# Explicit per-engine instruction lists for a fused attention and MLP kernel

## The chip, the cores and the metric

The kernel runs on one core of a Trainium2 chip. The metric is the device time of one execution in microseconds, as a median of several runs. The core has five engines that take their instructions from queues of their own, each strictly in order: TensorE (PE, matrix products), ScalarE (ACT, functions such as exp), VectorE (DVE, elementwise work), GpSimd (POOL) and SyncE (SP), which here only issues transfers. An instruction at the head of a queue that waits for another engine holds everything behind it in that queue. So the order within each queue, which is fixed when the program is built, decides how well the engines overlap.

## What is computed

Eight batches, eight heads, 576 tokens, head size 64. A small packed set of 32 queries `p` attends to the keys and values, its result serves as keys and values for the queries `q`, and the result of that goes through an MLP with a swish whose slope is a vector.

```python
def sm_attn(qq, kk, vv):
    s = scale * np.matmul(qq, kk.transpose(0, 1, 3, 2))
    s = s - np.max(s, axis=-1, keepdims=True)
    a = np.exp(s)
    a = a / (np.sum(a, axis=-1, keepdims=True) + 1e-09)
    return np.matmul(a, vv)
p_packed = sm_attn(p, k, v)              # p: 8 x 8 x 32 x 64
out = sm_attn(q, p_packed, p_packed)     # q: 8 x 8 x 576 x 64
# x = out as (8*576) x 512
h = x @ w_in                             # 4608 x 2048
g = h * (1.0 / (1.0 + np.exp(-beta * h)))
y = g @ w_out                            # 4608 x 512
```

All inputs and the output are float32.

## The kernel before

The kernel multiplies `p_packed` into `w_in` first (tile `w_ps`, scaled by beta into `W_bf`), so that per batch `h_ps` is a product of `W_bf` and the attention weights `A2T`. It does 512 of a batch's 576 tokens as a main part and joins the remaining 64 of two batches (`hr_ps`, `g_rem`). For batches 2 to 7 the output product is one level of a seven-product scheme with sums of quarters of `w_out` (`w_sum`) and of `g` (`g_sum`); batches 0 and 1 use plain products, batch 0 in two halves of `w_out`.

Every piece of work is a task with a key, such as `("A2", 1, 0)`, an engine or several to choose from, an estimated duration, and the tasks that it depends on. The names that matter here:

- `ld`, `ld_in`, `ld_out`: loads of q, k, v and the two weights; `cast`: float32 to bf16 of q, k, v; `w_in`, `w_out`: casts of the weights; `tr`: transposes of k and q (by DMA from batch 2 on)
- `s1`, `e1`, `z1`, `pun`, `pp`: scores, exp, sums, product and normalisation of the first attention; `s2`, `e2`, `z2`, `l2`, `n2`, `A2`: the same of the second
- `w`, `W`: product of `pp` with `w_in`, and its scaling; `h`, `g`: first MLP product and its silu; `hr`, `gr`: the same for the remaining tokens
- `o`: plain output products; `p`, `P`: the seven products; `S`, `T4`: sums of `g` and of `w_out`; `take`, `add`, `R..`: reading the output out of PSUM

A planner turns the tasks into the five queues. It plays the program through in a time model, and each time an engine is free it takes the ready task with the lowest rank:

```python
while todo:
    moved = False
    for e in ready:
        if free[e] > now + 1e-9:
            continue
        can = [t for t in ready[e] if t.ready <= now + 1e-9 and room(t.takes, t.count) and best(t, e)]
        # ... (ScalarE: function tables are switched here)
        if not can:
            if e == "PE" and warm - 1e-9 <= now < WARM_UNTIL and room("o", 1):
                self.filler()                  # a small matmul on no data of the problem
                free[e], warm = now + 0.06, now + WARM_US
                moved = True
            continue
        start(min(can, key=lambda t: t.rank), e)
        moved = True
    # ... (nothing moved: step to the next time)
```

The ranks are a formula by batch and kind plus a table of numbers, one for each task, that an earlier search left; a second table holds back some tasks, a third ties some to one engine:

```python
ORDER = { ('A2', 0, 0): 89.4, ('A2', 0, 1): -16.1, ('A2', 0, 2): -98.7, ... }   # some 900 numbers
AFTER = { ('A2', 6, 1): 184.56, ('P', 2, 2): 109, ... }
PIN = { ('R11', 5): 'DVE', ('cast', 1, 'k', 2): 'ACT', ... }

def task(self, key, engine, us, fn, deps=(), rank=0, **kw):
    deps = [self.tk.get(d) if isinstance(d, tuple) else d for d in deps]
    t = self.plan.add(engine, us, fn, deps, rank + ORDER.get(key, 0), **kw)
    t.key, t.ready = key, AFTER.get(key, 0.0)
    if key in PIN:
        t.any = {PIN[key]: t.any[PIN[key]]}
```

The casts of q, k and v for batches 2 to 7 are GpSimd's, one instruction for all eight heads and one for the remaining tokens:

```python
c0 = self.task(("cast", b, x, 0), "POOL", 1.95, lambda f=piece: f("POOL", 0, 8), [m0] + old, rank + 3)
self.tk["cast", b, x, 1] = c0
self.task(("cast", b, x, 2), "POOL", 0.4, lambda f=tail: f("POOL"), [mr, c0], rank + 3)
```

The four sums of `w_out` (`w_sum`) need all of `w_out` cast, and are read first by the products of batch 2. `A2` multiplies two tiles in SBUF; `W` reads one operand from PSUM:

```python
a, b = {1: (w(0, 1), w(0, 0)), 2: (w(1, 1), self.sum_w(1)), 3: (w(1, 1), w(0, 1)), 4: (w(1, 0), self.sum_w(2))}[i]
nc.vector.tensor_tensor(self.sum_w(i), a, b, ALU.subtract)                    # T4
nc.vector.tensor_tensor(part(st[b, "A2"], i), part(st[b, "E2"], i), ..rz2.., ALU.mult)   # A2
nc.vector.tensor_tensor(st[b, "W"][:, r, cols], st[b, "w", m][:], self.beta_bc[:, cols], ALU.mult)   # W
# h of batch b needs A2 (b, 0), A2 (b, 1), two of the eight W of batch b, and the bank ring "h" of two
```

PSUM is dealt out in rings: two banks for `h`, two for `o`, four for the attention (`att`). A task that opens a bank waits until the one that had it has been read out.

Of the kernel before, what the change touches and what calls it, by code (L numbers as in the profile page):

```python
# [8 lines left out]
B, H, S, D = 8, 8, 576, 64  # L9
# [6 lines left out]
bf16 = mybir.dt.bfloat16  # L16
# [27 lines left out]
HALVED = (0,)  # L44
PLAIN = (0, 1)
# [3 lines left out]
ORDER = {  # L49
    ('A2', 0, 0): 89.4, ('A2', 0, 1): -16.1, ('A2', 0, 2): -98.7, ('A2', 1, 0): 0.2, ('A2', 1, 1): -1,  # L50
    ('A2', 2, 0): 100, ('A2', 2, 1): 70, ('A2', 2, 2): 70, ('A2', 3, 0): -22, ('A2', 3, 1): -23.7, ('A2', 3, 2): -19,
    ('A2', 4, 0): -16.6, ('A2', 4, 1): -3, ('A2', 4, 2): 72, ('A2', 5, 0): 7.7, ('A2', 5, 1): 5.4, ('A2', 5, 2): 3.7,
    ('A2', 6, 0): -36.4, ('A2', 6, 1): -66.7, ('A2', 6, 2): -10.7, ('A2', 7, 0): 185.4, ('A2', 7, 1): -153.6,
    ('A2', 7, 2): -86.6, ('P', 2, 1): -5.7, ('P', 2, 2): -0.9, ('P', 2, 4): -7, ('P', 2, 5): -474.2,
    ('P', 2, 6): -1.8, ('P', 2, 7): -462.9, ('P', 3, 2): 6.4, ('P', 3, 3): -14.7, ('P', 3, 4): -32.4,
    ('P', 3, 5): -33, ('P', 3, 6): -455.7, ('P', 3, 7): -464.5, ('P', 4, 1): 0.6, ('P', 4, 2): -464.5,
    ('P', 4, 3): -110.3, ('P', 4, 5): 5.1, ('P', 4, 6): -457, ('P', 4, 7): -439.9, ('P', 5, 1): -75,
    ('P', 5, 4): -433.3, ('P', 5, 5): 0.6, ('P', 5, 6): -461.4, ('P', 5, 7): -400.6, ('P', 6, 1): 7,
    ('P', 6, 2): -582.1, ('P', 6, 3): 25.1, ('P', 6, 5): -573.1, ('P', 6, 6): -514.9, ('P', 6, 7): -65.7,
    ('P', 7, 1): -67.6, ('P', 7, 2): 6.1, ('P', 7, 3): 0.6, ('P', 7, 4): -18, ('P', 7, 5): -0.9, ('P', 7, 6): 3.7,  # L60
    ('R11', 2): 78, ('R11', 3): -87, ('R11', 4): 97.2, ('R11', 5): 30.3, ('R11', 6): -6.4, ('R11', 7): 30.6,
    ('R11+', 2): -30.6, ('R11+', 3): 54.4, ('R11+', 4): 135.6, ('R11+', 5): 18.8, ('R11+', 6): 123, ('R11+', 7): 18.3,
    ('R12', 2): -42.6, ('R12', 3): -15, ('R12', 4): 0.7, ('R12', 5): -31.9, ('R12', 6): -1.3, ('R12', 7): -8.6,
    ('R12+', 2): 37, ('R12+', 3): -80.4, ('R12+', 4): 45, ('R12+', 5): 30, ('R12+', 6): 95, ('R12+', 7): -123.6,
    ('R21', 2): -121, ('R21', 3): 14, ('R21', 4): 30, ('R21', 5): -9.3, ('R21', 6): -53, ('R21', 7): 60,
    ('R22', 2): 0.3, ('R22', 3): 62.3, ('R22', 4): -1.7, ('R22', 5): -16.7, ('R22', 6): 9.4, ('R22', 7): -28.2,
    ('R22+', 2): -9.4, ('R22+', 3): 15.6, ('R22+', 4): -16, ('R22+', 5): 13.8, ('R22+', 6): 0.6, ('R22+', 7): 3,
    ('S', 2, 1): -12, ('S', 2, 2): -10.7, ('S', 2, 3): -5, ('S', 2, 4): -12, ('S', 3, 1): -4.3, ('S', 3, 2): -34.3,
    ('S', 3, 3): 2.7, ('S', 3, 4): -64.3, ('S', 4, 1): -61.3, ('S', 4, 2): -99.3, ('S', 4, 3): -106.3,
    ('S', 4, 4): -109.3, ('S', 5, 1): -235.9, ('S', 5, 2): 60, ('S', 5, 3): 83, ('S', 5, 4): 57, ('S', 6, 2): 60,  # L70
    ('S', 6, 3): 60.3, ('S', 6, 4): 57, ('S', 7, 1): 68.6, ('S', 7, 2): 71.6, ('S', 7, 3): 71.6, ('S', 7, 4): -3.4,
    ('T', 0, 'k', 0): 75, ('T', 0, 'k', 1): 75, ('T', 0, 'q', 0): 76.3, ('T', 0, 'q', 1): 75, ('T', 1, 'k', 0): 60.6,
    ('T', 1, 'k', 1): 90.6, ('T', 1, 'q', 0): 60.6, ('T', 1, 'q', 1): 60.6, ('T4', 1): -210.4, ('T4', 2): -73.5,
    ('T4', 3): -72.8, ('T4', 4): 15, ('W', 0, 0): -31.7, ('W', 0, 1): -30, ('W', 0, 2): -30, ('W', 0, 3): -30,
    ('W', 0, 4): -23, ('W', 0, 5): -30, ('W', 0, 6): 75.6, ('W', 0, 7): -11, ('W', 1, 0): -2.4, ('W', 1, 1): -35.1,
    ('W', 1, 2): 25, ('W', 1, 3): -90, ('W', 1, 4): -60, ('W', 1, 5): -53, ('W', 1, 6): -60.6, ('W', 1, 7): -60,
    ('W', 2, 0): -118.7, ('W', 2, 1): 57, ('W', 2, 2): 1.3, ('W', 2, 3): -30, ('W', 2, 4): 3, ('W', 2, 5): -60,
    ('W', 2, 6): -1.9, ('W', 2, 7): 13.7, ('W', 3, 0): -61.7, ('W', 3, 1): -61.7, ('W', 3, 2): -61.7,
    ('W', 3, 3): -30.4, ('W', 3, 4): -68.7, ('W', 3, 5): -91.7, ('W', 3, 6): -58.7, ('W', 3, 7): -60.4,
    ('W', 4, 0): 13, ('W', 4, 1): 73, ('W', 4, 2): -2, ('W', 4, 3): 12.4, ('W', 4, 4): 13.6, ('W', 4, 5): 13,  # L80
    ('W', 4, 6): -161.4, ('W', 4, 7): 28, ('W', 5, 0): 30, ('W', 5, 1): 26, ('W', 5, 2): 40.6, ('W', 5, 3): 30,
    ('W', 5, 4): 37, ('W', 5, 5): 30, ('W', 5, 6): 37, ('W', 5, 7): 31.3, ('W', 6, 0): 46, ('W', 6, 1): 84.3,
    ('W', 6, 2): 24.3, ('W', 6, 3): 54.3, ('W', 6, 4): -65.7, ('W', 6, 5): -49.3, ('W', 6, 6): 54, ('W', 6, 7): 51.7,
    ('W', 7, 0): 63, ('W', 7, 1): -57, ('W', 7, 2): 3, ('W', 7, 3): 3, ('W', 7, 4): 3, ('W', 7, 5): 3, ('W', 7, 6): 3,
    ('W', 7, 7): 3, ('add', 0, 0): 36.6, ('add', 0, 1): 70.8, ('add', 0, 2): 52, ('add', 0, 3): 37, ('b_safe',): 11,
    ('bcol',): -7, ('beta', 0): 67, ('beta', 1): 50, ('beta', 3): 36.4, ('brow', 0): 16.6, ('brow', 1): 14,
    ('brow', 2): -38.6, ('brow', 3): 180, ('cast', 0, 'k', 0): -80.9, ('cast', 0, 'k', 1): -49.2,
    ('cast', 0, 'k', 2): -73.9, ('cast', 0, 'q', 0): -13.9, ('cast', 0, 'q', 1): -80.3, ('cast', 0, 'q', 2): -80.9,
    ('cast', 0, 'v', 0): -78.3, ('cast', 0, 'v', 1): -20.9, ('cast', 0, 'v', 2): -83.9, ('cast', 1, 'k', 0): -76.7,
    ('cast', 1, 'k', 1): -76.7, ('cast', 1, 'k', 2): -76.7, ('cast', 1, 'q', 0): -76.7, ('cast', 1, 'q', 1): -83.7,  # L90
    ('cast', 1, 'q', 2): -147.4, ('cast', 1, 'v', 0): -23.9, ('cast', 1, 'v', 1): -76.7, ('cast', 1, 'v', 2): -76.7,
    ('cast', 2, 'k', 0): 88.7, ('cast', 2, 'k', 2): 28.7, ('cast', 2, 'q', 0): -1.3, ('cast', 2, 'q', 2): 29.3,
    ('cast', 2, 'v', 0): 58.7, ('cast', 2, 'v', 2): 31.7, ('cast', 3, 'k', 0): -0.7, ('cast', 3, 'k', 2): 1.2,
    ('cast', 3, 'q', 0): 0.6, ('cast', 3, 'q', 2): 37.6, ('cast', 3, 'v', 0): 7.9, ('cast', 3, 'v', 2): 60.6,
    ('cast', 4, 'k', 0): -53.6, ('cast', 4, 'k', 2): 3.4, ('cast', 4, 'q', 0): 6.4, ('cast', 4, 'q', 2): 8.3,
    ('cast', 4, 'v', 0): 21.4, ('cast', 4, 'v', 2): -38.6, ('cast', 5, 'k', 0): -5.3, ('cast', 5, 'k', 2): 60.4,
    ('cast', 5, 'q', 0): -25.9, ('cast', 5, 'q', 2): 31.7, ('cast', 5, 'v', 0): -43.3, ('cast', 5, 'v', 2): -1.9,
    ('cast', 6, 'k', 0): -16.3, ('cast', 6, 'k', 2): -0.7, ('cast', 6, 'q', 0): -1.3, ('cast', 6, 'q', 2): -1.3,
    ('cast', 6, 'v', 0): -1.3, ('cast', 6, 'v', 2): -15.7, ('cast', 7, 'k', 0): 7.6, ('cast', 7, 'k', 2): 0.6,
    ('cast', 7, 'q', 0): 0.6, ('cast', 7, 'q', 2): -14.4, ('cast', 7, 'v', 0): 0.6, ('cast', 7, 'v', 2): 0.6,  # L100
    ('e1', 0, 0): -61.9, ('e1', 0, 1): -1.9, ('e1', 1, 0): -326, ('e1', 1, 1): -326.3, ('e1', 2, 0): 26.1,
    ('e1', 2, 1): -391, ('e1', 3, 0): -59, ('e1', 3, 1): -44, ('e1', 4, 0): 98, ('e1', 4, 1): -4, ('e1', 5, 1): 13.7,
    ('e1', 6, 0): -30.7, ('e1', 6, 1): -31.3, ('e1', 7, 0): 60.6, ('e1', 7, 1): 60, ('e1r', 0): 68, ('e1r', 1): -29.4,
    ('e1r', 2): -388, ('e1r', 3): -11.4, ('e1r', 4): -60.6, ('e1r', 5): 5.3, ('e1r', 6): -38.9, ('e1r', 7): -32,
    ('e2', 0, 0): 7, ('e2', 0, 1): 69.8, ('e2', 1, 0): -68.3, ('e2', 1, 1): -7.3, ('e2', 2, 0): 41.1,
    ('e2', 2, 1): 48.7, ('e2', 3, 0): -6.4, ('e2', 3, 1): -375.3, ('e2', 4, 0): -80.9, ('e2', 4, 1): -80.3,
    ('e2', 5, 0): 67, ('e2', 5, 1): 7, ('e2', 6, 0): -46.2, ('e2', 6, 1): -46.5, ('e2', 7, 0): 52.4,
    ('e2', 7, 1): -14.6, ('e2r', 0, 0): -7.7, ('e2r', 0, 1): -8.3, ('e2r', 1, 0): 53.3, ('e2r', 1, 1): -3.7,
    ('e2r', 2, 0): -47.4, ('e2r', 2, 1): -47.4, ('e2r', 3, 0): -58.7, ('e2r', 3, 1): -58.1, ('e2r', 4, 0): 5.1,
# [177 lines left out]
    ('w', 3, 2): 99.46, ('w', 6, 1): 175.13, ('w', 6, 2): 183.08, ('w', 7, 1): 203.14,  # L287
}
PIN = {
    ('R11', 5): 'DVE', ('cast', 1, 'k', 2): 'ACT', ('w_in', 0, 1): 'POOL', ('w_out', 4): 'DVE',  # L290
}


# [17 lines left out]
class Planner:  # L311
# [14 lines left out]
    def run(self):  # L326
# [4 lines left out]
        for t in self.tasks:  # L331
            t.left = len(t.deps)
            for d in t.deps:
                d.users.append(t)
# [1068 lines left out]
```

## Time and profile before

| what | value |
|---|---|
| time, median of 3 runs | 260.38 us (260.34 to 261.25) |
| span of the profiled execution | 259.6 us |
| TensorE matmul busy | 235.8 us, 91% |
| ScalarE busy | 173.5 us, 67%, of which 26 table loads 33.4 us |
| VectorE busy | 162.0 us, 62% |
| GpSimd busy | 53.0 us, 20% |
| moved by DMA | 54.11 MB, mean 208 GB/s |

A profile's page cuts the span into 40 slices of 6.5 us and gives for each engine a digit, its busy share in tenths; a second row gives the clock that TensorE was granted. Other views answer for one stretch of time: busy time by stage, a timeline of the instructions of an engine (start, length, what it is, and in brackets how long the engine had been idle before it and what ended that), the waits summed by who waited for whom, and the chain of waits that ended last. Matmuls overlap one another, so a busy TensorE isn't one at its peak; idle time of an engine that isn't the bound costs nothing.

### The profile page before, as it was taken

What the parts mean: (1) busy time and instruction counts of PE and PEld (TensorE: products, weight loads), DVE (VectorE), ACT (ScalarE), POOL (GpSimd) and SP (SyncE); (2) the same over time, 40 slices, a digit from 0 to 9 for tenths busy, and PEclk for the clock granted to TensorE, in tenths of its full rate; (3) what the DMA queues carried; (4) which work ended last, traced back from release to release, by engine and by line L of the source; (5) the groups of instructions that cost most, each with busy time, mean ns of one, the idle gap of its engine ahead of it and who ended that gap; (6) DMA issues with size and microseconds to landing.
All of it is one profiled execution on the core that took longest, in us unless ns stands there. A gap on an engine that the chain in (4) does not pass through costs nothing.

```text
span 259.6 us, 5648 instructions
## 1 busy us (share of the span) xinstructions
PE 235.8 (91%) x2338; PEld 149.1 (57%) x2367; DVE 162.0 (62%) x245; ACT 173.5 (67%) x311; POOL 53.0 (20%) x51
## 2 busy tenths in 40 slices
PE   3995897785999999999999999999999999999993
PEld 2972344541344454478468646677567845767971
DVE  5768587999826546467637783664577488522621
ACT  3266749975286686688778878877786768656210
POOL 4022200038233006303510550054400000000000
PEclk9999999998699999999999999999999999999998
DMA  6999999999949599979969993998994021103122
GB/s 204 322 362 378 376 286 285 328 286 232 280 146 213 134 293 310 211 200 305 229 169 297 296 168 112 308 278 206 277 176 89 3 83 81 42 3 141 63 78 83
DMA packets 74825, 54.11 MB, mean 208 GB/s; under 512 B 42688, under 2 KB 68304, under 8 KB 74800
## 3 DMA queue, kind: packets, MB, share of 16 engines
q1 hardware_dynamic: 74496, 53.68, 78.0%
q8 instruction: 18, 0.29, 0.5%
q10 hardware_dynamic: 304, 0.07, 0.1%
q14 instruction: 7, 0.06, 0.1%
HBM read 37.23 MB, written 9.44 MB: 180 GB/s over the span
## 4 chain that ended last, share of the span: by engine, by line
PE 71%; DMA 14%; DVE 5%; ACT 5%; SPq 2%; POOL 1%; issue 1%
PE o_ps L448 40%; PE h_ps L448 19%; DMA w_in<-in_moe_w_in_dram 8%; DMA w_out<-in_moe_w_out_dram 5%; PE w_ps L448 3%; PE hr_ps L448 2%; DVE w_sum L1046 2%; DMA k<-in_k_dram 2%; PE s_ps L448 2%; PE z_ps L448 2%; ACT L463 1%; PE pp_ps L448 1%; ACT g_main L894 1%; POOL w_in_bf L1310 1%; DVE W_bf L862 1%
## 5 line engine op out<-in xcount | busy, mean ns | idle before, releaser
L894 ACT ACTIVATE g_main<-h_ps 128x512 bf16<-128x512 f32 x128 | 72.8, 596 | 40.1 <-PE h_ps L448 35.0
L448 PEld LDWEIGHTS <-g_main 128*128 128x128 bf16 x608 | 56.6, 98 | 31.5 <-issue 9.0
L448 PE MATMUL o_ps<-w_out_bf,g_main 128*128 128x256 bf16 (+1 forms) x409 | 72.5, 309 | 2.2 <-DVE w_out_bf L1321 1.6
L448 PE MATMUL h_ps<-A2T,W_bf 128*128 128x512 bf16 x238 | 70.4, 386 | 3.3 <-ACT g_main L894 1.5
L862 DVE TENSOR_TENSOR W_bf<-w_ps,beta_bc 128x512 bf16<-128x512 f32 x64 | 41.6, 684 | 15.5 <-PE w_ps L448 15.0
L448 PEld LDWEIGHTS <-W_bf 128*128 128x128 bf16 x512 | 32.4, 98 | 24.1 <-issue 10.5
L463 ACT ACT_TABLE_LOAD x26 | 33.4, 1283 | 1.1 <-PEq L1387 0.7
L448 PE MATMUL o_ps<-w_sum,g_main 128*128 128x256 bf16 x192 | 26.5, 273 | 0.2
L1102 DVE TENSOR_TENSOR o_sb<-o_ps,o_sb 128x512 f32<-128x512 f32 x18 | 12.4, 689 | 22.3 <-PE o_ps L448 17.3
L448 PE MATMUL o_ps<-w_sum,g_sum 128*128 128x256 bf16 x192 | 25.1, 273 | 0.1
L531 POOL CAST q_bf<-q 128x2048 bf16<-128x2048 f32 x6 | 11.9, 1988 | 46.4 <-DMA q<-in_q_dram 26.2
L448 PEld LDWEIGHTS <-g_sum 128*128 128x128 bf16 x192 | 18.4, 98 | 4.3 <-issue 0.2
L1104 DVE COPY o_sb<-o_ps 128x512 f32<-128x512 f32 x13 | 9.0, 690 | 17.1 <-PE o_ps L448 17.1
L448 PE MATMUL w_ps<-w_in_bf,pp 64*32 64x512 bf16 x256 | 13.7, 386 | 4.9 <-DVE W_bf L862 2.0
L448 PEld LDWEIGHTS <-pp 64*32 64x32 bf16 x384 | 5.6, 89 | 20.2 <-issue 16.8
L803 DVE TENSOR_TENSOR A2T<-E2T,rz 128x512 bf16<-128x512 bf16 x16 | 12.2, 770 | 6.6 <-ACT rz L798 6.6
L448 PE MATMUL o_ps<-w_out_bf,g_rem 128*128 128x512 bf16 x61 | 15.5, 380 | 0.4 <-ACT o_sb L1104 0.2
L531 POOL CAST v_bf<-v 128x2048 bf16<-128x2048 f32 x6 | 11.6, 1931 | 14.2 <-PE pp_ps L448 5.5
L531 POOL CAST k_bf<-k 128x2048 bf16<-128x2048 f32 x6 | 11.6, 1934 | 11.7 <-DMA k<-in_k_dram 10.0
L914 ACT ACTIVATE g_rem<-hr_ps 128x512 bf16<-128x512 f32 x16 | 9.5, 598 | 5.3 <-PE hr_ps L448 5.2
L1104 ACT COPY o_sb<-o_ps 128x512 f32<-128x512 f32 x11 | 6.4, 585 | 8.6 <-PE o_ps L448 8.5
L1072 DVE TENSOR_TENSOR g_sum<-g_main 128x2048 bf16<-128x2048 bf16 x6 | 7.3, 1220 | 7.6 <-ACT g_main L894 7.6
(96 smaller groups left out, 267.2 us busy)
## 6 DMA issues: line engine op xcount, KB each, us to landing
out_dram<-o_sb SPq DMA_DIRECT2D x14, 512.0 KB, 3.0
k<-in_k_dram SPq DMA_DIRECT2D x6, 1024.0 KB, 8.8
v<-in_v_dram SPq DMA_DIRECT2D x6, 1024.0 KB, 7.7
q<-in_q_dram SPq DMA_DIRECT2D x6, 1024.0 KB, 7.8
w_in<-in_moe_w_in_dram SPq DMA_DIRECT2D x4, 1024.0 KB, 8.4
w_out<-in_moe_w_out_dram SPq DMA_DIRECT2D x4, 1024.0 KB, 10.6
k<-in_k_dram SPq DMA_DIRECT2D x4, 512.0 KB, 7.3
q<-in_q_dram SPq DMA_DIRECT2D x4, 512.0 KB, 6.9
```

Source lines behind the costliest of these rows:

```text
L448: return self.nc.tensor.matmul(out, lhsT, rhs, start=start, stop=stop, tile_position=pos, skip_group_check=True)
L463: self.nc.scalar.preload_act_table_set(SETS[mode])
L531: self.copy[engine](o[:, 0:2048].rearrange("p (t h d) -> p h t d", t=4, h=8)[:, h], t[:, 0:2048].rearrange("p (h t d) -> p h t d", h=8, t= ...
L803: nc.vector.tensor_tensor(part(st[b, "A2"], i), part(st[b, "E2"], i), st[b, "rz2"][:, i] if i < 2 else st[b, "rz2r"][:], ALU.mult)
L862: nc.vector.tensor_tensor(st[b, "W"][:, r, cols], st[b, "w", m][:], self.beta_bc[:, cols], ALU.mult)
L894: nc.scalar.activation(st[b, "g"][:, ft, :], st[b, "h", ft][:], AF.Silu)
L914: nc.scalar.activation(st[b // 2, "gr"][:, 8 * half : 8 * half + 8, o : o + 64], st[b, "hr", half][:].rearrange("p (f n) -> p f n", f=8), ...
L1046: nc.vector.tensor_tensor(self.sum_w(i), a, b, ALU.subtract)
L1072: nc.vector.tensor_tensor(o, x, y, op)
L1102: nc.vector.tensor_tensor(o, x, o, ALU.add)
L1104: self.copy[engine](o, x)
L1310: self.copy[engine](self.w_in_bf[:, c, 512 * n : 512 * n + 512], self.t["w_in", n][:, c])
```

## The change

The tables of ranks, delays and ties go. In their place stands one list of task keys for each engine, found by a search over sequences. The planner takes each engine's tasks in the order of its list, and keeps a time model only to interleave the five lists when it writes the program and to place fillers in TensorE's gaps. The model, which the search used too, now knows that VectorE's work within SBUF (the kinds in `PORT`) and GpSimd's work exclude each other. The GpSimd casts of batches 2 to 7 are cut in two halves of four heads. Some dependencies that the old planner got from its order by rank are now stated.

```diff
+PORT = ("S", "T4", "A2", "cast", "w_in", "w_out", "p_dup", "p0_bf")
-ORDER = { ... }
-AFTER = { ... }
-PIN = { ... }
+SEQUENCE = {
+    "PE": [ ("brow", 0), ("tr", 0, "k", 0), ("p0_tr", 0), ("brow", 1), ... ],
+    ...
+    "DVE": [ ...
+        ("take", 0, 3), ("W", 1, 0), ("w_out", 12), ("w_out", 15), ("w_out", 14), ("W", 1, 1), ("rq", 1),
+        ("add", 0, 1), ("A2", 1, 0), ("A2", 0, 2), ("add", 0, 0), ("A2", 1, 1), ("W", 1, 2), ("W", 1, 3), ("T4", 1),
+        ("W", 1, 4), ("W", 1, 5), ("add", 0, 2), ("add", 0, 3), ("T4", 2), ("pT1", 0), ("W", 1, 6), ("pT1", 0, 1),
+        ("A2", 1, 2), ("pT1", 1, 1), ("T4", 3), ("W", 1, 7), ... ],
+    "POOL": [ ... ],
+    "SP": [ ... ("ld_out", 1), ("ld_in", 3), ("ld", 1, "q", 0), ("ld", 1, "v", 0), ("ld", 1, "v", 1), ("ld", 1, "v", 2),
+        ("ld", 1, "q", 1), ("ld_out", 2), ("ld_out", 3), ("ld", 1, "q", 2), ("ld", 2, "k", 0), ("ld", "p"),
+        ("ld", 2, "v", 0), ("ld", 2, "k", 2), ("ld", 2, "q", 0), ("ld", 2, "q", 2), ("ld", 2, "v", 2),
+        ("tr", 2, "k", 0), ... ],
+}
     # Planner.run
+        named = {t.key: t for t in self.tasks}
+        todo = {e: [named.pop(k) for k in keys] for e, keys in SEQUENCE.items()}
+            if e == "POOL":
+                at = max(at, held["DVE"] - 0.12)
+            elif e == "DVE" and t.port:
+                at = max(at, held["POOL"] - 0.12)
+            for _ in range(int((min(at, WARM_UNTIL) - free["PE"]) / WARM_US)):
+                self.filler()
     # casts of batches 2 to 7
-                c0 = self.task(("cast", b, x, 0), "POOL", 1.95, lambda f=piece: f("POOL", 0, 8), [m0] + old, rank + 3)
-                self.tk["cast", b, x, 1] = c0
+                c0 = self.task(("cast", b, x, 0), "POOL", 0.97, lambda f=piece: f("POOL", 0, 4), [m0] + old, rank + 3)
+                self.task(("cast", b, x, 1), "POOL", 0.97, lambda f=piece: f("POOL", 1, 4), [m0, c0], rank + 3)
     # dependencies now stated, for example
-                [h, ("g", b, 0) if ft else None], rank, ends=[h], table="silu",
+                [h], rank, ends=[h], table="silu",
```

Compared as instruction orders, the two programs have the same matmuls except for the fillers (70 before, 38 after), 26 and 24 table loads on ScalarE, 183 and 174 rows on VectorE, 56 and 68 on GpSimd. In the old order of VectorE three of the four `w_sum` come before the first `A2` of batch 1; in the new one both `A2` and four of the eight `W` of batch 1 come before the first `w_sum`. On the load queue the tensor p of the later batches moves from before the last two quarters of `w_out` to behind them.

## The prediction

> **What bounds the kernel now.** I read the page's slices first, then busy time by stage, then the timeline of VectorE and GpSimd in the one stage that stood out, then the chain of waits. The slices (6.5 us each):
>
> ```profile
> PE   3995897785999999999999999999999999999993
> ...
> PEclk9999999998699999999999999999999999999998
> DMA  6999999999949599979969993998994021103122
> ```
>
> TensorE is full from about 66 us to the end; before that it has holes in nearly every slice, and the clock row dips once, in slices 10 and 11 (58 to 71 us). The weights and the first two batches come in over the first 52 us, with the DMA row at 9. Busy time by stage (columns: length, then busy us and count of PE, PEld, DVE, ACT, POOL, then clock, DMA share, GB/s):
>
> ```profile
> 40.00:54.00 14.00, 10.14 (x130) 6.54 (x130) 11.78 (x23) 12.20 (x19) 1.05 (x2) 1.00 1.09 305
> 54.00:65.00 11.00, 7.83 (x92) 3.16 (x91) 10.97 (x13) 7.70 (x17) 7.08 (x6) 0.90 1.19 250
> ...
> 100.00:150.00 50.00, 49.59 (x540) 32.65 (x530) 32.45 (x47) 38.98 (x73) 15.77 (x15) 1.00 1.02 249
> ```
>
> From 54 to 65 us VectorE is busy 10.97 of 11 us: it, and no longer the loads, is the bound there. The same view in steps of 2 us shows what follows:
>
> ```profile
> 60.00:62.00 2.00, 0.40 (x8) 0.12 (x7) 1.98 (x4) 1.29 (x3) 1.31 (x2) 1.00 1.07 311
> 62.00:64.00 2.00, 1.04 (x9) 0.30 (x9) 2.00 (x2) 0.00 (x0) 1.87 (x2) 0.68 1.48 114
> 64.00:66.00 2.00, 1.98 (x6) 0.62 (x5) 2.00 (x3) 0.60 (x1) 1.66 (x1) 0.50 1.18 281
> 66.00:68.00 2.00, 2.00 (x6) 0.66 (x5) 2.00 (x3) 0.73 (x2) 0.23 (x1) 0.50 0.81 257
> 68.00:70.00 2.00, 2.00 (x7) 0.78 (x6) 1.13 (x3) 0.47 (x1) 0.40 (x1) 0.61 0.85 228
> ```
>
> TensorE stands still (0.40 of 2 us), and then runs at half clock until about 69 us. Lost to the clock: 0.32 x 2 + 0.5 x 4 + 0.39 x 2 = 3.4 us. The timelines of VectorE and GpSimd say why VectorE is late:
>
> ```profile
> 55.95 1.21 DVE L1046 TENSOR_TENSOR w_sum<-w_out_bf,w_sum 128x2048 bf16<-128x2048 bf16 x1
> 57.09 2.90 DVE L1046 TENSOR_TENSOR w_sum<-w_out_bf 128x2048 bf16<-128x2048 bf16 x1
> ...
> 60.63 0.68 DVE L803 TENSOR_TENSOR A2T<-E2T,rz 128x512 bf16<-128x512 bf16 x1
> ...
> 61.83 1.78 DVE L803 TENSOR_TENSOR A2T<-E2T,rz 128x512 bf16<-128x512 bf16 x1
> ```
> ```profile
> 56.78 2.14 POOL L531 CAST k_bf<-k 128x2048 bf16<-128x2048 f32 x1 [2.76 <-DMA k<-in_k_dram]
> 58.87 1.39 POOL L541 CAST k_bf<-kr 128x256 bf16<-128x256 f32 x1
> 60.95 2.12 POOL L531 CAST v_bf<-v 128x2048 bf16<-128x2048 f32 x1 [0.69 <-DMA v<-in_v_dram]
> ```
>
> The same operation takes 1.21 us alone and 2.90 us beside a GpSimd cast, 0.68 and 1.78 us for the other. In the chain of waits these pieces follow one another, w_sum for 3.96 us, W_bf, A2T for 1.70 us, and only at 63.66 us the h_ps that starts the dense part.
>
> **What the Trainium skill says.** "SBUF — State Buffer", section "SBUF: two separate sides", says that VectorE and GpSimd share a port pair as an exclusive lock, taken by a VectorE operation with two SBUF inputs or in a two-port mode; the loser waits for the other's whole instruction. The trace agrees (the pairs above; W_bf, which reads PSUM, stays at 0.69 us beside a cast). "TensorE: Matmul & The Clock Gate", Part 1, says the clock falls to half after idleness and comes back after a busy window of some 3.4 us; here it is 0.50 after the 2 us hole and back after some 6. "ScalarE: Activation LUTs", section "What ACT_TABLE_LOAD costs", gives 1283 ns; the trace has 1283.
>
> **The change, part by part.**
>
> *Same work.* By the two instruction orders, TensorE does the same matmuls but for fillers, 38 against 70. ScalarE has 24 table loads for 26 (2 x 1.28 = 2.6 us less), VectorE 174 rows for 183: three more w_out casts go to ScalarE, the small bias arithmetic and one cast of p to GpSimd. None of this is the bound after 66 us.
>
> *Casts in halves.* 18 GpSimd casts of 1.9 us become 36 of 128x1024, which the trace has once undisturbed at 1.04 us: +0.2 us each pair, 3.4 us in all on an engine at 20%, so free. A VectorE operation then waits at most about 1 us, not 1.9.
>
> *VectorE's order between 50 and 66 us.* Now all of w_out is cast, three w_sum are made (5.3 us), and then come W_bf and A2T of batch 1, on which h of batch 1 waits. The list puts both A2T and four of the eight W_bf of batch 1 ahead of the first w_sum; the four w_sum are spread over batch 1, since batch 2 reads them first.
>
> *When h of batch 1 can start.* In the loads' order p (384 KB) moves behind w_out, 1.3 us at 300 GB/s; VectorE first waited for the last w_out until 52.49 us, so estimate 51.2. Behind it the list has on VectorE three w_out at 0.44, W_bf 0.6, a small copy 0.25, two adds and two A2T at 0.6, a small A2T 0.2: 1.3 + 0.6 + 0.25 + 2.4 + 0.2 = 4.8 us, so 56.0. The list alternates with TensorE and ScalarE here (an add waits for its product, the product two tiles on waits for the bank the add frees, A2T for the logarithm and exponential of about 0.6 us each), some six hand-overs of 0.2 to 0.3 us: estimate **57 to 59, I take 58**. TensorE has products of batch 0 to do meanwhile, so it should not cool.
>
> *What remains then.* Before, the last matmul ends at 255.2 us. From 66 us on that is 189.2 us, of which 1.0 + 0.8 us were lost to the clock: 187.4 at full clock. By counts, what the old order had done at 66 and the new order has not when h of batch 1 starts: two or three h matmuls (0.5), 32 hr (0.94), 16 transposes of p (0.9); the other way, some eight output matmuls (1.7). Net +0.6: 188.0 us. 58 + 188.0 = 246.0, plus the tail after the last matmul as now (259.6 - 255.2 = 4.4): span 250.4. Time minus span is 0.8 now: 251.2.
>
> *The rest of the run.* From 70 to 255 us TensorE is 93 to 100% busy in every 10 us; the largest hole is 0.7 us, at 185 to 195. But busy overstates use. In the chain two h matmuls follow each other every 0.43 us and four half-width ones every 0.44: 221 h and 142 full-width output matmuls at 0.215, 672 half-width ones at 0.109 and about 28 us of small ones come to some 180 of the 187 us. A search with truer durations can win 1 to 3 of the 7; a fixed order that misjudges the chip can lose as much. I add 0.8 as the price of new stalls: **252.0**.
>
> **Rivals.**
> *The loads stay the bound, and nothing but the clock loss returns.* For: the DMA row is 9 to 52 us. If h of batch 1 still starts at 62, with TensorE warm, the time is about 256. Against: between 52.5 and 63.7 us nothing that TensorE waits for is in flight.
> *Batch 2 becomes late instead.* Its k is loaded behind w_out, cast on GpSimd and transposed by DMA (kT issued at 60.28 us for 3.95); its queue now also carries p and more remainder loads ahead. The list asks for its scores about 12 us after h of batch 1 starts, near 70 us; the transpose could land at 67 to 72. That costs 0 to 3 us: up to 255. Later DMA shares near 1.0 (100 to 150 us) speak for it; holes of 3 to 6 tenths against.
> *The lists misfit the chip.* Queues are taken in order, so one late operation holds those behind it; VectorE's casts and GpSimd's may still meet. A second cold stretch costs about 3.4 us. Times of 255 to 260; slower than now needs several of these.
>
> **Range and chances.** Start of h in batch 1 at 55 to 62 gives -3 to +4; the steady part -3 to +3: range 248 to 257. 2% faster is 255.2, inside the upper part of the range: faster 0.84, same 0.13, slower 0.03.
>
> **What would show it.** Right: no w_sum over 1.4 us before h of batch 1; that h at 57 to 59; no clock stretch at 0.5 near 62 to 70; TensorE 9 from slice 8 or 9 on; the last matmul near 246. Wrong: h of batch 1 after 61, TensorE waiting at 68 to 75 for scores of batch 2, a new clock dip, or more than 2 us more idle between 100 and 230.

## The result, and the profile after

The changed kernel takes **251.59 us** (median of 4 runs, 250.85 to 252.77) against 260.39 us for the kernel before beside it: a ratio of 0.966, 95% interval 0.962 to 0.970. Predicted were 252.0 us, in a range of 248 to 257.

The slices of the page after, 6.2 us each, with the rows that were shown of before:

```profile
PE   2974899999999999999999999999999999999992
...
PEclk9997589999999999999999999999999999999998
DMA  6999999999999999999498999899491631004122
```

Counted from 1, the hole of slices 8 to 10 (7, 8, 5) and the dip of the clock in slices 10 and 11 are gone: TensorE is at 9 from slice 6 on, sooner than the 8 or 9 that were predicted. There is a dip that before did not have, in slices 4 to 6 (22.3 to 32.6 us by the mean clock of 2 us stretches), while the weights are still coming in.

Busy time by stage (length, then busy us and count of PE, PEld, DVE, ACT, POOL, then clock, DMA share, GB/s):

```profile
24.00:32.00 8.00, 6.92 (x38) 3.98 (x39) 6.15 (x11) 4.89 (x7) 0.00 (x0) 0.50 1.08 342
...
40.00:54.00 14.00, 13.37 (x130) 6.26 (x130) 12.95 (x26) 11.88 (x23) 0.00 (x0) 1.00 1.10 314
54.00:65.00 11.00, 10.79 (x88) 4.94 (x84) 9.71 (x14) 8.57 (x17) 5.38 (x5) 1.00 1.20 246
...
100.00:150.00 50.00, 49.73 (x552) 33.59 (x556) 35.00 (x51) 38.72 (x72) 16.20 (x18) 1.00 1.01 244
```

TensorE is busy 10.79 of 11 us where it was busy 7.83, and 13.37 of 14 where it was busy 10.14. From 100 to 150 us it was full and is full.

The timeline of VectorE after, at the place where before had two `w_sum` and two slow `A2T`, and GpSimd's:

```profile
53.83 0.68 DVE L733 TENSOR_TENSOR A2T<-E2T,rz 128x512 bf16<-128x512 bf16 x1
...
55.30 0.68 DVE L733 TENSOR_TENSOR A2T<-E2T,rz 128x512 bf16<-128x512 bf16 x1
56.41 1.29 DVE L792 TENSOR_TENSOR W_bf<-w_ps,beta_bc 128x512 bf16<-128x512 f32 x2 [0.43 <-PE w_ps L380]
57.62 1.59 DVE L983 TENSOR_TENSOR w_sum<-w_out_bf 128x2048 bf16<-128x2048 bf16 x1
```
```profile
56.10 2.03 POOL L461 CAST k_bf<-k 128x1024 bf16<-128x1024 f32 x2 [16.37 <-PE z2r_ps L380]
58.07 2.03 POOL L1168 CAST p_dup<-p 96x1024 bf16<-96x1024 f32 x1
```

No `w_sum` stands ahead of the two `A2T`, which take 0.68 us each, ahead of the first of GpSimd's casts. The longest `w_sum` is now 1.91 us, at 62.47 us.

In TensorE's timeline h of batch 1 runs from 57.59 us. Before, its very first matmul came at 62.31 us and the second waited for the second `A2T` until 63.66; this second time is the one that the prediction took as the start, and that is compared here. The scores of batch 2 follow with no wait ahead of them. Before, then after:

```profile
62.31 0.39 PE L448 MATMUL h_ps<-A2T,W_bf 128*128 128x512 bf16 x1
63.66 0.58 PE L448 MATMUL h_ps<-A2T,W_bf 128*128 128x512 bf16 x1 [0.96 <-DVE A2T L803]
```
```profile
57.59 1.04 PE L380 MATMUL h_ps<-A2T,W_bf 128*128 128x512 bf16 x4
...
68.88 0.63 PE L380 MATMUL s_ps<-pT,kT 128*128 128x64 bf16 x16
```

The last matmuls end at 245.02 us, before at 255.17: 10.15 us sooner. The chain of waits after, summed by engine, is this line of the page (before: PE 71%, DMA 14%, DVE 5%):

```profile
PE 82%; DMA 10%; ACT 4%; issue 1%; DVE 1%; SPq 0%
```

Followed in order of time, the chain leaves the loads at 27.35 us (`k` of batch 1) and then runs over TensorE and a few pieces of ScalarE; before, a load of `w_out` was on it until 52.47 us. In the repetition of the changed kernel (below) the chain is still on a load of `w_in` until 38.93 us, so the loads are not far from it.

Where the time went can be put into a ledger for 40 to 70 us, worked out from the two kernels' tables of stages: TensorE idle, TensorE on fillers, and time at a lowered clock.

| 40 to 70 us | before | after |
|---|---|---|
| idle (40-54, 54-58, 58-70) | 3.86 + 0.22 + 2.94 = 7.0 us | 0.63 + 0.16 + 0.11 = 0.9 us |
| fillers | 1.8 us | 0.2 us |
| clock (0.72 over 12 us) | 3.4 us | 0 |
| sum | 12.2 us | 1.1 us |

The difference, 11.1 us, covers the 10.15. Some 0.5 us of it is counted twice, since the hole of 0.96 us before 63.66 us lies in the stretch at half clock, and the ledger isn't exact to 1 us: a busy TensorE is not one at its peak.

The groups behind the row of fillers show a part of the change that is easily overlooked. Output products of batch 0 and fillers from 40 to 54 us, before and then after:

```profile
L448 PE MATMUL o_ps<-w_out_bf,g_main 128*128 128x512 bf16 x14 | 3.8, 378 | 1.6 <-DVE w_out_bf L1321 1.6
L448 PE MATMUL o_ps<-identr 128*128 128x128 bf16 x18 | 1.8, 220 | 0.1
```
```profile
L380 PE MATMUL o_ps<-w_out_bf,g_main 128*128 128x512 bf16 x28 | 8.0, 380 | 0.2 <-issue 0.2
L380 PE MATMUL o_ps<-identr 128*128 128x128 bf16 x1 | 0.2, 219 | 0.0
```

In the stretch in which before put 18 fillers and 14 output products, after runs 28 output products and one filler. (These are records; a few are missing in both traces. By the lists, 48 output products of batch 0 stand ahead of the first h of batch 1 before, and 58 after.)

### The profile page after: what moved, and what is told of

Read it like the earlier page. It is cut to its first block, busy times and chain, and to the rows that moved or that the text cites. A ratio compares the mean times of both kernels' runs of the same rounds, so it can differ in the third digit from the quotient of the medians.

```text
span 249.5 us, 5593 instructions
## 1 busy us (share of the span) xinstructions
PE 232.3 (93%) x2306; PEld 147.7 (59%) x2335; DVE 155.1 (62%) x236; ACT 174.6 (70%) x313; POOL 60.6 (24%) x74
## 4 chain that ended last, share of the span: by engine, by line
PE 82%; DMA 10%; ACT 4%; issue 1%; DVE 1%; SPq 0%
PE o_ps L380 45%; PE h_ps L380 22%; DMA k<-in_k_dram 7%; PE w_ps L380 4%; PE hr_ps L380 3%; DMA v<-in_v_dram 3%; PE z_ps L380 2%; ACT L395 2%; PE s_ps L380 2%; PE pp_ps L380 2%; ACT g_main L823 1%; PE kT_ps L385 1%; ACT E1T L583 1%; PE s2r_ps L380 0%; PE pT_ps L385 0%
## 5 line engine op out<-in xcount | busy, mean ns | idle before, releaser
L380 PE MATMUL o_ps<-w_out_bf,g_main 128*128 128x256 bf16 (+1 forms) x410 | 71.3, 305 | 0.9 <-issue 0.5
L380 PE MATMUL h_ps<-A2T,W_bf 128*128 128x512 bf16 x237 | 69.7, 389 | 1.4 <-DVE A2T L733 0.9
L461 POOL CAST q_bf<-q 128x1024 bf16<-128x1024 f32 x14 | 15.1, 1084 | 30.0 <-DMA q<-in_q_dram 30.0
L461 POOL CAST v_bf<-v 128x1024 bf16<-128x1024 f32 x12 | 12.8, 1073 | 33.0 <-PE h_ps L380 12.8
L461 POOL CAST k_bf<-k 128x1024 bf16<-128x1024 f32 x12 | 12.2, 1043 | 25.8 <-PE z2r_ps L380 16.4
L380 PE MATMUL o_ps<-w_out_bf,g_rem 128*128 128x512 bf16 x60 | 16.1, 379 | 0.3 <-issue 0.2
L716 ACT ACTIVATE rz<-z_ps 128x512 f32<-128x512 f32 x16 | 9.5, 594 | 2.1 <-PE z_ps L380 2.0
```

What stands on the lines that cost most here:

```text
L380: return self.nc.tensor.matmul(out, lhsT, rhs, start=start, stop=stop, tile_position=pos, skip_group_check=True)
L461: self.copy[engine](o[:, 0:2048].rearrange("p (t h d) -> p h t d", t=4, h=8)[:, h], t[:, 0:2048].rearrange("p (h t d) -> p h t d", h=8, t= ...
L716: nc.scalar.activation(st[b, "rz2"][:, i], ps[:], AF.Ln)
```

## The experiments

The theory of the prediction: the new order takes `w_sum` out of the way of `A2` and `W` of batch 1, so h of batch 1 starts sooner and TensorE does not cool; the halves are free; the place of p's load is worth 1.3 us; the rest of the new lists brings nothing. The rival: much of the gain is in the rest of the searched order. "Old lists" is the kernel before with its order written out as explicit lists, which gives the same program (the traces of runs that change one engine's list have the same order of instructions on the others); "new lists" are those of the changed kernel. Each run had the kernel before beside it, at 260.3 to 261.1 us.

### The sums of w_out alone, in both directions

Old lists, with the four additions into `w_sum` moved:

```diff
-("w_out", 12), ("T4", 1), ("A2", 0, 2), ("T4", 2), ("T4", 3), ("W", 1, 0), ("A2", 1, 0), ...
+("w_out", 12), ("A2", 0, 2), ("W", 1, 0), ("A2", 1, 0), ...
+# T4 1 behind W (1, 3), 2 behind add (0, 3), 3 behind W (1, 7), 4 behind W (2, 3)
```

> The kernel before with its own five orders written out as lists, changed in one thing: on VectorE the sums of w_out (w_sum, 5.3 us in a row at 54.6 to 60.0 us) go behind W and A2 of batch 1, as the new list has them. Theory (the sums held back h of batch 1, and the hole they made cost the clock too): h of batch 1 starts near 60 us for 63.7, no stretch at half clock after 60 us, time 252 to 256, that is -4 to -8 us. Rival (the gain lies in the sum of many small shifts of the search, or in the order of the loads): -3 us or less.

Measured 256.22 us, ratio 0.984 (0.978 to 0.989): -4.8 us. TensorE's timeline and the stage view:

```profile
60.69 0.59 PE L389 MATMUL h_ps<-A2T,W_bf 128*128 128x512 bf16 x2 [0.60 <-ACT g_rem L853]
```
```profile
54.00:65.00 11.00, 10.22 (x106) 4.71 (x106) 8.34 (x13) 9.42 (x20) 5.86 (x5) 1.00 1.17 252
```

h starts 3.0 us sooner, the clock stays at 1.00, every `w_sum` takes 1.21 us. This one move alone brings half of the gain.

New lists, with the first three additions put back right behind the last cast of `w_out`:

> The changed kernel with one thing undone: the first three sums of w_out come right behind the last cast of w_out on VectorE, ahead of W and A2 of batch 1. Theory: h of batch 1 starts 4 to 5 us later than 57.6, some of the sums are stretched by GpSimd casts, TensorE has a hole of 3 us or more and cools; time 256 to 260, +5 to +8 us. Rival (other parts of the lists carry the gain): +2 us or less, 252 to 254.

Measured 256.89 us, ratio 0.983 (0.979 to 0.987), 5.0 us over the changed kernel's 251.87 (its repetition, below). The longest wait of TensorE from 50 to 64 us, this time at a score product whose copy of q (`qTr`) stands behind the three additions, and the stages behind it:

```profile
PE s2r_ps L380 <- DVE qTr L538: 3.2, 1, 3.2
```
```profile
54.00:56.00 2.00, 0.00 (x0) 0.00 (x0) 2.00 (x3) 0.59 (x1) 0.22 (x1) 1.00 1.08 252
...
58.00:60.00 2.00, 2.00 (x14) 0.66 (x12) 2.00 (x4) 0.00 (x0) 1.26 (x1) 0.50 1.14 268
```

The old picture comes back: VectorE busy 2.00 of 2 us, TensorE at 0.00, and then half clock. Both directions agree at 5 us. That remains the largest single part, and it is as large as it is because the wait also cools TensorE.

### The casts in halves, in both directions

Old lists, GpSimd's casts of batches 2 to 7 in two halves as in the change:

> The kernel before with its own orders as lists, and only the 18 whole GpSimd casts of batches 2 to 7 cut in halves, one behind the other. Theory (halves matter only as shorter waits for the shared port): the sum of 2.90 us and the A2T of 1.78 us at 57 to 64 us shrink by up to 1 us each, time -0 to -2 us. Rival (halves are the main part of the gain): -4 us or more. Second rival (VectorE is let in after each half no sooner): no change.

Measured 258.71 us, ratio 0.990 (0.986 to 0.994): -2.3 us by the medians. VectorE's timeline:

```profile
57.17 2.05 DVE L988 TENSOR_TENSOR w_sum<-w_out_bf 128x2048 bf16<-128x2048 bf16 x1
...
61.19 1.41 DVE L745 TENSOR_TENSOR A2T<-E2T,rz 128x512 bf16<-128x512 bf16 x1
```

The two were 2.90 and 1.78 us. A shorter cast makes the shorter wait, h starts 1.0 us sooner (62.66), and the half clock lasts 3.4 us instead of 6.8 (by the mean clock of 2 us stretches), which is 1.7 us of clock. So by these sums most of what the halves bring here comes by way of the clock.

New lists with whole casts, and the changed kernel itself again in the same set of runs:

> The changed kernel with whole GpSimd casts again, each at the place of its first half. Theory (casts are off the path, halves only shorten waits): within -0.5 and +1.5 us of the changed kernel; single VectorE operations beside a cast wait up to 1.9 us. Rival (halves carry the gain): +3 us or more.

> The changed kernel itself once more, as the base of the three beside it: 251 to 252.5 us.

Measured 253.67 us (251.85 to 254.75), ratio 0.971 (0.967 to 0.975), and 251.87 us, ratio 0.965 (0.962 to 0.968). The intervals overlap slightly, so the 1.8 us between them are likely, not certain. The longest `w_sum` is 2.52 us, and h starts at 58.17, no later than with halves (57.59 and 58.31): what whole casts cost comes after the start of h. TensorE waits 0.6 us twice, at 112 and 115 us, behind a sum of `g` that takes 2.91 us beside a whole cast (1.22 in the repetition) and an `A2T` of 1.79. So the two directions give like sizes, but from different places.

### The load of p

New lists, p's load put ahead of the last two quarters of `w_out`:

```diff
-("ld_out", 2), ("ld_out", 3), ("ld", 1, "q", 2), ("ld", 2, "k", 0), ("ld", "p"),
+("ld", "p"), ("ld_out", 2), ("ld_out", 3), ("ld", 1, "q", 2), ("ld", 2, "k", 0),
```

> The changed kernel with the load of p (384 KB) ahead of the last two loads of w_out, as before. Theory (arrival of w_out is what the start of h of batch 1 hangs on): w_out lands 1.3 us later, h of batch 1 starts 1 to 1.3 us later, time +1 to +1.3 us. Rival (VectorE's and ScalarE's chains behind the loads have room): less than +0.4 us.

Measured 255.17 us, ratio 0.978 (0.975 to 0.981): 3.3 us over the changed kernel run beside it. VectorE's timeline shows the last casts of `w_out`:

```profile
55.20 1.28 DVE L1258 TENSOR_SCALAR w_out_bf<-w_out,rbeta 128x512 bf16<-128x512 f32 x3 [0.87 <-DMA w_out<-in_moe_w_out_dram]
```

They start at 51.23 us in the profile of after and at 51.95 in its repetition, so p, 384 KB, holds the load stream up by 3.3 to 4.0 us, and h starts at 61.56. The estimate of 1.3 us, worked out from 300 GB/s, was too small by more than half.

The other direction, old lists with p's load moved back, could not be done by one move: the scores of batch 2 and the remainder product of batch 0 read what is made of p. The first try left p's doubling (`p_dup`) on VectorE, behind four `W` of batch 1; a second kernel had the sums late and the halves as well.

> The lists of the kernel before, with the load of p moved behind w_out and k of batch 2, as the changed kernel has it; what reads p (its doubling, its two transposes and their copies, and the remainder matmuls of batch 0, which share a buffer with it) stands later by as little as the dependences ask. w_sum stays ahead of W and A2 of batch 1. If p costs the load stream about 3 us, the last w_out lands that much sooner (near 49 to 50 us), the block of w_sum starts sooner, and the time falls by 2 to 3 us, to 258 to 259. If it costs 1.3 us, 259.5 to 260. Rival: p's own work on VectorE now falls in the crowded stretch of 54 to 65 us and eats the gain: 260.4 or more.

> The lists of the kernel before with three things changed at once: additions into w_sum behind W and A2 of batch 1, casts of GpSimd in halves, load of p behind w_out. If these three are what the new lists bring, and the searched order of the rest brings nothing, the parts measured alone (-4.8, -2.3, about -3) add up to nearly the whole gain: 251 to 254, h of batch 1 starting at 57 to 59.5, last matmul near 245 to 248. If they overlap (halves matter less once w_sum is out of the way), 253 to 255. Rival: the rest of the searched order carries a part, above all between 60 and 245 us: then this kernel stays above 255.

Measured 270.3 us, ratio 1.035 (1.031 to 1.040), and 267.4 us, ratio 1.028 (1.024 to 1.032): both slower than before. TensorE's timeline in the second:

```profile
65.03 0.82 PE L394 MATMUL pT_ps<-identr,p_dup 96*128 96x96 bf16 x8 [4.19 <-DVE p_dup L1170]
```

The load did what was expected (VectorE's wait for the last `w_out` ends at 50.41 us instead of 52.49 in the first of the two, 2.1 us sooner) and h of batch 1 starts at 57.85 us in the second. But TensorE takes its list in order: the transposes of p, put after the third h, waited 4.2 us for VectorE, half clock followed, and another 3.7 us were lost at a wait for silu. The rival that was named, p's work in the crowded stretch of VectorE, was right, and the loss was larger than it said.

So the third kernel had p's chain planned as the change has it, one half of the doubling on GpSimd and one on ScalarE, the transposes and the scores a few h later.

> As the run with all three changes on the old lists, but with the chain of p planned as the changed kernel plans it: its doubling on GpSimd (behind the two half casts of k of batch 2) and on ScalarE (behind the fourth silu of batch 1) instead of on VectorE, its transposes after the sixth and eighth h matmul pair of batch 1, the scores of batch 2 and the remainder matmuls of batch 0 two pairs later. In the run before this, h of batch 1 started at 57.85 us, as early as in the changed kernel, and all that was lost came in one wait of TensorE of 4.2 us for the doubling on VectorE with half clock behind it, and one of 3.7 us for silu. If that chain alone was the fault, the dense part runs through from 58 us and the time is 251 to 254. Rival: something else in the old order needs the early p, or the rest of the searched order carries the gain: 256 or more, with TensorE waits between 58 and 80 us that are not the doubling of p.

Measured 258.01 us, ratio 0.989 (0.987 to 0.991). That is a miss, and less of a gain than the sums alone brought (4.8 us). TensorE's timeline and its largest wait from 40 to 110 us:

```profile
58.31 0.88 PE L390 MATMUL h_ps<-A2T,W_bf 128*128 128x512 bf16 x2
```
```profile
PE w_ps L390 <- ACT E1T L612: 1.0, 1, 1.0
```

h starts at 58.31 us, where it starts in the repetition of the changed kernel too; the clock stays at 1.00; and still the time is 6.1 us longer than that one's. The last matmul ends at 251.65 us, 5.9 us later than in the repetition (245.75). Some 1.4 us are holes between 70 and 78 us, which come from where the chain of p was placed. By the lists, this kernel has run 48 output products of batch 0 when h starts, the changed one 58 (fillers in all: 70 and 38); the ten are some 2.15 us at 0.215. Another 1.3 us come late: at the scores of batch 4 both kernels have the same matmuls left, and from there this one needs 136.64 us to the last matmul, as the kernel before does (136.63), the repetition 135.38. About 1 us stays open. So the start of h is not the whole measure: what TensorE has left to do at that moment counts as well.

### The open work, tried by itself

New lists, in which only output products of batch 0 move from ahead of h of batch 1 to behind its fourth h (the text on record says fifth):

```diff
-... ("o", 0, 2, 9), ("o", 0, 2, 11), ("o", 0, 2, 13), ("z2", 1, 2), ("w", 1, 1), ("o", 0, 3, 9), ("o", 0, 3, 11), ("w", 1, 2), ("h", 1, 1), ...
+... ("z2", 1, 2), ("w", 1, 1), ("w", 1, 2), ("h", 1, 1), ("h", 1, 3), ("h", 1, 0), ("w", 1, 3), ("h", 1, 2), ("o", 0, 2, 9), ("o", 0, 2, 11), ...
```

> The lists of the changed kernel, with ten output matmuls of batch 0 (five pairs, 2.15 us at 0.215) taken from ahead of the first h of batch 1 to behind its fifth, and six more of the same group a little later; nothing else moves. It asks whether the start of h of batch 1 sets the end, as the prediction had it, or the amount of TensorE's work still open at that moment, as the run with the three changes on the old lists (h at 58.31 us, but 258.0) suggests. If the start is what counts, h starts at 57 to 58.5 and the time stays within 0.5 us of the changed kernel, 251.3 to 252.3 (ratio 0.963 to 0.967). If the open work counts, h starts no later, TensorE idles or runs fillers ahead of it, and the time rises by 1.5 to 2.5 us, to 253 to 254.3 (ratio 0.971 to 0.976).

Measured 254.24 us, ratio 0.975 (0.972 to 0.979): 2.4 to 2.7 us over the changed kernel, at the upper edge of what open work was to cost. TensorE's timeline:

```profile
56.91 1.04 PE L380 MATMUL h_ps<-A2T,W_bf 128*128 128x512 bf16 x4
```

h of batch 1 starts 0.7 us **sooner** than in the changed kernel, and the run is longer. The start of h follows from when its inputs are there; the end depends on how much work was left over for afterwards as well. Not all of the loss is that work. The last matmul ends at 247.95 us, 2.9 us after the first profile of the changed kernel and 2.2 after its repetition: the ten products are 2.15 us, the earlier start takes 0.7 off, and TensorE waits some 1.1 us that it did not wait before, for silu at 58.76 us and 0.42 us for p's doubling at 61.5:

```profile
58.76 0.59 PE L380 MATMUL h_ps<-A2T,W_bf 128*128 128x512 bf16 x2 [0.64 <-ACT g_main L823]
```

### The cold stretch at 22 to 33 us

Fillers placed every 0.1 us of a gap instead of every 0.3 (135 for 38):

```diff
-WARM_US = 0.3
+WARM_US = 0.1
```

> The changed kernel with fillers in TensorE's gaps up to 60 us every 0.1 us of the model for every 0.3 us, 135 for 38. In the profile TensorE is at half clock from 22.6 to 33.7 us, after a hole at 19 to 22. Theory (that cold stretch is hidden behind the loads): clock 1.0 or a shorter dip at 22 to 34, time within 0.5 us. Rival (TensorE's lag from the cold stretch reaches h of batch 1): -1 to -2 us.

Measured 253.11 us (251.81 to 253.76), ratio 0.969 (0.965 to 0.972). Half clock lasts from 21.9 to 25.3 us only, and nothing is gained: h of batch 1 starts at 57.62 us, against 57.59 and 58.31 in the two profiles of the changed kernel. In this kernel's chain the last load of `w_out` is back, from 39.78 to 51.23 us; in the changed kernel's first profile the chain leaves the loads at 27.35 us, in its repetition at 38.93. The reading that fits is that a warm TensorE only waits longer for the same loads. The run does not isolate it, since the 97 further fillers take TensorE's time too, and 0.67 us are lost later, at 79.9 us, at a wait for a transpose of q. That the stretch is harmless holds as long as the loads end no sooner.

## Why the prediction was right, and which terms were not

**The bound in the old kernel: right.** VectorE from 54 to 65 us, and the clock behind it. The sums moved alone give -4.8 us and put back +5.0; no stretch at half clock is left near 62 to 70.

**The lock between VectorE and GpSimd: right.** In the Trainium skill, "SBUF — State Buffer", section "SBUF: two separate sides", the loser waits for the other's whole instruction. With casts halved, the worst `w_sum` falls from 2.90 to 2.05 us and the worst `A2T` of that stretch from 1.78 to 1.41, as that reading asks; in the changed kernel an `A2T` ahead of the casts takes 0.68, and one beside them up to 1.52.

**h of batch 1 at 57 to 59: right**, 57.59 and 58.31. The last `w_out` casts start at 51.23 us against 51.2 estimated, and the last `A2T` ends at 55.98 against 56.0.

**188.0 us from there to the last matmul: right**, 187.4. The term came out because the prediction counted what each order had and had not done of TensorE's work by then (some eight output products more on the new side). But it stood there as a correction of 0.6 us, and what was to decide was the start of h alone. The runs give this term a size of its own: TensorE, while VectorE prepares h, has output products of batch 0 to run and runs them. With ten of them left for later, and the waits that came with it, 2.4 to 2.7 us are lost, and the three moves without the rest of the order bring 2.7 us and not 9.

**The halves as free: the size was off.** On GpSimd they are free (busy 60.6 us for 53.0, with a cast of p added). But the text gave them no gain of their own, and they are worth about 2 us in either direction (2.3 and 1.8, the second not certain).

**p's load at 1.3 us: mis-sized.** 2.1 us where it was taken out of the old stream, 3.3 us of time and more at the loads where it was put into the new one. It did not show in the total, because the landing it was used for was met, 51.23 for 51.2. The 300 GB/s came from a stretch of mostly large loads; by its measured cost p's came to less.

**0.8 us for new stalls: not seen.** From 40 to 100 us TensorE waits 0.9 us in all. **1 to 3 us from a better order of the rest: at the lower end.** From the scores of batch 4 on, with the same matmuls left, before needs 136.63 us to the last matmul and after 135.37, and 0.8 us of that are two waits of TensorE, of 0.56 us at 191.7 and 0.24 at 251.3, that are gone. The prediction named this term, set it against an equal loss, and left it out of its sum.

**Time minus span, 0.8 us: mis-sized.** It set the median of before against the span of a run that was slower than the median. That run took 261.44 us for its 259.6, and the profiled run of after 251.31 for 249.5: 1.8 us both times. That the total came within 0.4 us is therefore in part luck: 1 us too little here, against 0.8 us for stalls that did not come, 0.4 at the start of h and 0.6 from there on.

**The rivals.** Loads as the bound: not as that rival put it, since h starts at 58 and not at 62; but the loads are close, for 3 us of delay at `w_out` came through in full (3.3 us). Batch 2 late: its scores start at 68.88 us with no wait ahead. Lists that misfit the chip: a new clock dip, one of the signs of being wrong that the prediction named, did come, at 22 to 33 us, where the text had not foreseen it, and it cost nothing that a run could show.

The parts overlap and are not to be added: 4.8 to 5.0 (sums), 1.8 to 2.3 (halves), about 3 (p), 2.4 to 2.7 (output products), 1.3 (late order) come to more than 9. Each is measured with the others held as they are in one of the two kernels.

## What to carry to other kernels

When one start is late, ask two things, not one: what it waits for, and what the engine that sets the end does meanwhile. A schedule that brings the start forward by leaving other work of that engine for later has gained nothing; count that engine's instructions up to the start in both orders. And a load that is moved takes its whole chain along: in queues that are taken in order, a consumer left in its old place turns a gain of 2 us into a loss of 10.

## What the hardware showed that was not expected

**The half clock lasts whole steps of some 3.4 us.** The stage view gives its ends, for the changed kernel and then for the one with 135 fillers:

```profile
22.00:24.00 2.00, 0.81 (x11) 0.19 (x8) 1.43 (x3) 0.41 (x1) 0.00 (x0) 0.58 1.06 365
...
32.00:34.00 2.00, 2.00 (x9) 0.88 (x8) 1.50 (x3) 1.29 (x2) 0.00 (x0) 0.86 1.06 375
```
```profile
20.00:22.00 2.00, 0.72 (x14) 0.49 (x14) 0.00 (x0) 0.80 (x2) 1.23 (x2) 0.98 1.05 315
22.00:24.00 2.00, 1.85 (x20) 1.09 (x17) 1.43 (x3) 0.41 (x1) 0.00 (x0) 0.50 1.06 365
24.00:26.00 2.00, 2.00 (x25) 1.56 (x25) 2.00 (x4) 0.17 (x1) 0.00 (x0) 0.67 1.10 356
```

A mean of 0.58 is half clock for 1.68 of 2 us, so it runs from 22.3 to 32.6 us, 10.2 us; with the fillers from 21.9 to 25.3, 3.4 us; in the kernel before, by the lines in the prediction, from 62.7 to 69.6, 6.8 us. In all thirteen traces every such stretch ahead of the last matmul has one of these three lengths. They are three times, once and twice the busy window of some 3.4 us that the Trainium skill gives in "TensorE: Matmul & The Clock Gate", Part 1. How full TensorE must be for the clock to return is not shown: the new lists with whole casts had the same hole of 0.9 us near 26 us as the repetition of the changed kernel, and came back after 6.8 us where that took 10.2. As an estimate from these lengths, a hole that cools TensorE takes 1.7, 3.4 or 5.1 us of full clock from it.

**A small load can cost more than its bytes.** 384 KB of p, 96 rows, cost the load stream 2.1 to 4.0 us, an estimate of 100 to 190 GB/s from these numbers, in a stream that otherwise moved 314 GB/s (40 to 54 us).

**A low clock on TensorE for ten microseconds cost nothing that showed**: with it (22.3 to 32.6 us) h of batch 1 started at 57.59 and 58.31 us, without most of it at 57.62.
